# Window attention with sink keys and a gated feed-forward block on one core: sink values by transfer, paired sink products, an uneven last block and a new order of work

## The chip, the cores and the metric

The kernel runs on one core of a Trainium2 chip. The core has a matrix engine (TensorE, "PE" in the profile, with its weight loads shown apart as "PEld"), VectorE ("DVE"), ScalarE ("ACT"), GpSimd ("POOL") and SyncE ("SP"), which run their own instruction queues in order and wait for each other by semaphores. Transfers are started by POOL, SP and ACT and carried out by 16 DMA engines. Matrix products land in eight accumulator banks of 128 x 512 float32. The metric is the device time of one execution, in microseconds; the lower the better.

## What is computed

Attention over 4 batches, 8 heads, 768 positions and head size 64. Each query sees the last 128 keys up to itself, and the first four keys of the sequence (the "sinks"). Its output, 3072 rows of 512, is normalized by its root mean square and goes through a gated feed-forward block with 1536 hidden columns.

```python
scores = scale * np.matmul(q, k.transpose(0, 1, 3, 2))
is_sink = pos[None, :] < int(n_sink)            # 4
in_window = (rel >= 0) & (rel < int(window))    # 128
scores = np.where(is_sink | in_window, scores, -1e9)
a = softmax(scores)
x = np.matmul(a, v)           # heads side by side: 3072 x 512
xn = x / rms * rms_g
g = xn @ w_gate
silu = g * (1.0 / (1.0 + np.exp(-g)))
out = (silu * (xn @ w_val)) @ w_out
```

## The kernel before

The work is cut into 24 blocks of 128 query rows, `g` = 0 to 23, six to a batch (`NT` = 6; `b` is the batch, `t` the block's place in it). A block's q, k and v come by transfers that GpSimd issues (L400, L404) and that turn float32 into bfloat16; k and q of block 0 come through SP as float32 instead (L392) and are cast. The first eight blocks are transposed on TensorE (L492), later ones by transposing transfers on SP (L506). The weights `wg`, `wv` and `wo` come through GpSimd as well (L446, L452), between the first blocks.

Scores are held transposed: keys on the partitions, queries along the columns. A block of keys meets its own queries and those of the next block. Three forms exist: the plain one (L532, tiles of 64 rows by 128 columns of the array, two heads side by side), one for a batch's last block (L548, the same tiles), and one that leaves the empty triangles out (L610, "tri", tiles of 64 by 64, used from block 4 on for all but a batch's first and last block). ScalarE takes exponentials (L583, L559, L619), VectorE or GpSimd masks them, and the products with v (`av`, L653 to L668) sum numerator and denominator, by a column of ones beside v. Each block has two halves of four heads, `u` = 0 and 1, each in one bank.

From a batch's third block on (`t` >= 2) the sinks lie outside the window and have a product of their own. `sink_s` (L772) gives the scores of the sinks, their exponentials are `esk` (L781), 128 partitions holding every head's sinks. `vsk` holds the values of the four sinks on the partitions that belong to each head, zero elsewhere. It is made by `sink_v` (L754), which multiplies v of the batch's first block with a selecting matrix `sel` on TensorE, once for each half, and by `sink_vm` (L763), in which VectorE multiplies the result with the mask `headm`. `sel` and `headm` are made once from the identity (L367, L371). The first product of `av` is then `esk` with `vsk`, 128 x 128 by 260 columns (L653), and starts the bank.

After `av`, VectorE divides (L682), ScalarE squares and sums (L690), VectorE normalizes (L697 to L714), and the block is transposed into `xnt`, by TensorE for the first eight blocks (L729) and by a transfer on SP for the others (L741). The feed-forward part works on groups of four blocks, `G` = 0 to 5. Its products `g` and `v` (both L1000) go in chunks of 128 columns for group 0, 256 for groups 1 and 2, and 512 for the others; ScalarE's tanh (L1007) and two passes of VectorE (L1013, L1023) turn them into `hT`; `project` (L1033) multiplies with `wo`, ScalarE evicts (L1041) and SP stores (L1045). The last block of all is projected in two halves of 256 columns (L1051), evicted by ScalarE and VectorE (L1062, L1066) and stored by ACT and SP (L1069).

What sets the order: every piece of work is an entry of a plan (`op`), with what it needs, what it gives, and which banks it takes and drops. The table `ORDER` lists, for each engine, the entries in the order in which that engine's queue gets them. `Plan.run` walks through these five lists with durations of its own to decide how they interleave in the program and which of the eight banks an entry gets. Thirty small products with zeros (`warm`, L468) stand among the first of TensorE's entries.

Of the kernel before, what the change touches and what calls it, by code (L numbers as in the profile page):

```python
# [9 lines left out]
ALU = mybir.AluOpType  # L10
# [5 lines left out]
P = 128  # L16
# [18 lines left out]
class Plan:  # L35
# [5 lines left out]
    LATE = 300  # L41
    DEPTH = 8
    WARM_AT = 11500
    HOP = {"PE": 40, "ACT": 35, "DVE": 35, "POOL": 90, "SP": 60}
    START = {"PE": 800, "ACT": 800, "DVE": 1030, "POOL": 1290, "SP": 800}

    def __init__(self):
        self.ops, self.held = [], {}
        self.rings = {"POOL": 0, "HW": 0, "TR": 0}
        self.banks = {i: 0 for i in range(8)}  # L50

    def op(self, ways, needs=(), gives=(), prio=0.0, takes=(), drops=(), ring=None, work=0.0,
           mode=0):
        self.ops.append(dict(
            ways=ways, needs=set(needs), gives=tuple(gives), prio=prio, takes=tuple(takes),
            drops=tuple(drops), ring=ring, work=work, mode=mode, at=len(self.ops), ready=0,
        ))

    def land(self, ring, first, work):


        r = self.rings
        if ring == "POOL":
            begin = max(first, r["POOL"], r["HW"])
            r["POOL"] = begin + (1.4 * work if begin < 8500 else work)
            self.loads -= 1
            return r["POOL"] + 520 + (1000 if r["POOL"] > 9000 else 0)
        if ring == "HW":
            begin = max(first, r["HW"], r["POOL"])
            r["HW"] = begin + (1.25 * work if begin > 2500 else work)  # L70
            return r["HW"] + 900
        begin = max(first, r["TR"])
        late = max(0, r["POOL"] - begin)
        if late and self.loads:
            r["POOL"] += 1.1 * work
        r["TR"] = begin + work
        return r["TR"] + (550 if ring == "TR" else 850) + min(late, 5000)

    def run(self, table):
        ids = {e: span(table[e]) for e in self.START}  # L80
        assert sorted(sum(ids.values(), [])) == list(range(len(self.ops)))
        free, at, users, last = dict(self.START), dict.fromkeys(self.START, 0), {}, []
        self.loads = sum(o["ring"] == "POOL" for o in self.ops)
        wait = {o["at"]: set(o["needs"]) for o in self.ops}
        for o in self.ops:
            for t in o["needs"]:
                users.setdefault(t, []).append(o)
        mode, order = 0, []
        lock, pool_end = (0, 0), 0
        while len(order) < len(self.ops):  # L90
            first = None
            for e in self.START:
                if at[e] == len(ids[e]):
                    continue
                o = self.ops[ids[e][at[e]]]
                k = len(o["takes"])
                if wait[o["at"]] or k > len(self.banks):
                    continue
                ready = o["ready"] + self.HOP[e] if o["ready"] else 0
                if k:  # L100
                    ready = max(ready, sorted(self.banks.values())[k - 1] + 40)
                if o["ring"] == "POOL" and len(last) >= self.DEPTH:
                    ready = max(ready, last[-self.DEPTH])
                start = max(free[e], ready)
                if first is None or start < first[0]:
                    first = start, e, o
            if first is None:
                raise RuntimeError("stuck")
            start, e, o = first
            at[e] += 1  # L110
            ns, lat, fn = o["ways"][e]
            if e == "PE":
                cold = max(0, self.WARM_AT - start)
                ns += min(ns, cold / 2)
                if o["mode"] != mode:
                    ns, mode = ns + 95, o["mode"]
                lat = ns + 180
            if o["mode"] == 9:
                if e == "DVE":
                    more = max(0, pool_end - (start + ns - 770))  # L120
                    lock = start + ns + more - 770, start + ns + more
                else:
                    more = lock[1] - start if start < lock[1] and start + ns > lock[0] else 0
                    pool_end = start + ns + more
                ns, lat = ns + more, lat + more
            for s in o["takes"]:
                i = min(self.banks, key=lambda i: (self.banks[i], i))
                del self.banks[i]
                self.held[s] = i
            free[e] = start + ns  # L130
            end = start + lat
            if o["ring"] is not None:
                end = self.land(o["ring"], end, o["work"]) + self.LATE
                if o["ring"] == "POOL":
                    last.append(end)
            for s in o["drops"]:
                self.banks[self.held[s]] = end + 12
            for t in o["gives"]:
                for x in users.pop(t, ()):
                    x["ready"] = max(x["ready"], end + 12)  # L140
                    wait[x["at"]].discard(t)
            order.append((start, end, e, fn, o))
        return order
# [21 lines left out]
""",  # L165
    "ACT": """
19 15 139 144 146 149 145 147 150 137 151 173 152 157 194 176 178 177 183 179 181 196
184 182 189 198 200 199 167 201 192 579 208 584 594 211 215 599 609 589 614 232 604 217
219 218 220 619 250 234 227 236-239 169 252 254 256 624 245 634 267 629 640 295 262 273
271 274 272 297 248 299-302 265 281 659 650 645 664 655 284 308 674 315 291 316 669 317  # L170
318 330 331 679 332 333 311 684 345 346 689 347 348 324 339 694 360 293 699 362 704 720
374 709 375 376 354 377 396 397 714 368 398 725 399 384 749 744 739 759 405 730 764 754
735 411-414 392 426-429 769 420 441 442 774 443 444 779 789 784 800 435 794 453 458 460
472-475 815 466 805 482 494 829 495 496 824 497 819 810 834 839 844 854 849 859 869 864
506 512-515 874 530 531 490 532 533 548 549 890 880 904 550 909 551 524 919 566 568 899
542 924 934 914 560 929 939 944 574 949 895 885 954 984 989 979 999 960 994 1009 975
1004 1014 1019 970 1029 1024 1034 965 1040 1050 1045 1053 1054
""",
    "DVE": """
7 0-2 11 10 17 6 141 12 171 4 13 163 156 154 158 165 213 5 186 188 160 161 190 202 203  # L180
# [23 lines left out]
""",  # L204
}


@with_exitstack
def kernel(
# [13 lines left out]
    nc = tc.nc  # L223
# [939 lines left out]
```

## Time and profile before

| | |
|---|---|
| median of 3 runs | 244.19 us (243.29 to 245.17) |
| the profiled execution | 242.75 us |
| its span, first to last instruction | 241.0 us |
| TensorE's granted clock, mean | 0.984 |
| DVE / ACT / POOL busy | 78% / 51% / 37% |
| L653, sink products, 128 x 260 | 32 instructions, mean 275 ns |
| L754, products with `sel`, 128 x 260 | 8 instructions, mean 306 ns |
| L763, `vsk` on VectorE, 128 x 260 | 8 instructions, mean 422 ns |

"PE busy" counts a matmul from its start to its modelled end, so that neighbours overlap; the distance from one start to the next tells how long a product holds the engine. The chain of waits is followed back from the last instruction, at each step to what released it. Line numbers are those of the kernel before.

### The profile page before, as it was taken

To read this page: it belongs to the slowest core of one execution; us is meant where nothing else is said; L and a number is where in the kernel's file an instruction comes from. 1 tells how busy PE (TensorE), PEld (TensorE's weight loads), DVE (VectorE), ACT (ScalarE), POOL (GpSimd) and SP (SyncE) were. 2 spreads that over 40 slices of the span, in tenths; PEclk is the share of its full clock that TensorE was granted. 3 is DMA by queue.
4 is the path that set the end of the run, shared out by engine and by line. 5 is a ranking of instruction groups with operands and counts; after the bars stand their busy time and mean duration, and the time that the engine had idled before them with its cause. 6 is when DMAs were issued, how large, how long until landed. Compare 5 with 4: busy or idle time off the path is not lost.

```text
span 241.0 us, 5846 instructions
## 1 busy us (share of the span) xinstructions
PE 235.0 (98%) x2324; PEld 149.8 (62%) x2324; DVE 187.0 (78%) x482; ACT 122.3 (51%) x267; POOL 89.9 (37%) x116
## 2 busy tenths in 40 slices
PE   6999999999999999999999999999999999999994
PEld 3469987875788676786886544445545444444443
DVE  2489979998999999999998999974599965436430
ACT  3775577477867565346754373461762222304211
POOL 8976885587555475200062123045340000000000
PEclk9679999999999999999999999999999999999999
DMA  9999999999999999999997809510241130103014
GB/s 125 148 183 188 184 184 187 164 136 150 141 137 149 180 165 146 159 180 169 141 153 70 109 0 112 115 40 0 87 47 22 21 112 0 69 18 131 3 50 167
DMA packets 113581, 27.38 MB, mean 114 GB/s; under 512 B 103697, under 2 KB 110609, under 8 KB 113554
## 3 DMA queue, kind: packets, MB, share of 16 engines
q0 software_dynamic: 81760, 13.90, 77.5%
q1 hardware_dynamic: 31650, 12.99, 29.8%
q8 instruction: 18, 0.29, 0.5%
q10 hardware_dynamic: 144, 0.13, 0.2%
q14 instruction: 9, 0.07, 0.1%
HBM read 28.31 MB, written 6.29 MB: 144 GB/s over the span
## 4 chain that ended last, share of the span: by engine, by line
PE 85%; DMA 7%; POOL 5%; issue 0%; DVE 0%; POOLq 0%
PE o L1033 25%; PE v L1000 24%; PE g L1000 23%; DMA wv<-in_moe_w_val_dram 4%; DMA q<-in_q_dram 3%; PE s L610 3%; PE av L668 2%; PE av L663 2%; PE av L653 2%; POOL wg L446 1%; POOL q L400 1%; POOL v L404 1%; PE o_last L1051 1%; POOL k L400 1%; PE s L532 1%; POOL wv L446 1%
## 5 line engine op out<-in xcount | busy, mean ns | idle before, releaser
L1000 PE MATMUL v<-xnt,wv 128*128 128x128 bf16 (+2 forms) x528 | 73.3, 282 | 0.0
L1000 PE MATMUL g<-xnt,wg 128*128 128x128 bf16 (+2 forms) x528 | 70.9, 282 | 0.0
L1033 PE MATMUL o<-wo,hT 128*128 128x512 bf16 x276 | 67.7, 379 | 0.0
L1007 ACT ACTIVATE th<-g 128x512 bf16<-128x512 f32 x72 | 41.6, 600 | 45.0 <-PE g L1000 40.0
L1013 DVE SCALAR_TENSOR_TENSOR p<-th,g 128x512 bf16<-128x512 bf16 x72 | 47.5, 682 | 17.6 <-ACT th L1007 17.4
L1000 PEld LDWEIGHTS <-wg 128*128 128x128 bf16 x528 | 43.2, 98 | 19.6 <-DMA wg<-in_moe_w_gate_dram 0.2
L1023 DVE TENSOR_TENSOR hT<-p,v 128x512 bf16<-128x512 bf16 x72 | 47.8, 682 | 9.6 <-PE v L1000 8.9
L1000 PEld LDWEIGHTS <-wv 128*128 128x128 bf16 x528 | 42.7, 98 | 19.9 <-issue 0.7
L1033 PEld LDWEIGHTS <-hT 128*128 128x128 bf16 x276 | 25.7, 98 | 26.0 <-issue 0.4
L644 POOL TENSOR_SCALAR_AFFINE_SELECT e<-e 128x512 bf16<-128x512 bf16 x20 | 12.6, 652 | 51.1 <-ACT e L619 50.8
L619 ACT ACTIVATE e<-s 128x384 bf16<-128x384 f32 x52 | 22.8, 498 | 15.4 <-PE s L610 15.3
L404 POOL DMA_DIRECT2D v<-in_v_dram x24 | 21.4, 890 | 9.1 <-DMA q<-in_q_dram 5.7
L690 ACT ACTIVATE sq<-x 128x512 bf16<-128x512 bf16 x24 | 15.3, 636 | 17.9 <-DVE x L682 17.7
L400 POOL DMA_DIRECT2D k<-in_k_dram x23 | 20.4, 888 | 8.5 <-DMA wo<-in_moe_w_out_dram 2.7
L400 POOL DMA_DIRECT2D q<-in_q_dram x23 | 20.5, 890 | 7.7 <-DMA k<-in_k_dram 4.5
L1041 ACT ACTIVATE osb<-o 128x512 f32<-128x512 f32 x23 | 13.5, 602 | 19.0 <-PE o L1033 19.0
L682 DVE TENSOR_TENSOR x<-av,rden 128x256 bf16<-128x256 f32 x48 | 20.4, 425 | 1.7
L714 DVE SCALAR_TENSOR_TENSOR xr<-x,r,gb 128x512 bf16<-128x512 bf16 x24 | 18.0, 752 | 0.8
L668 PE MATMUL av<-v,e 128*128 128x65 bf16 x192 | 17.8, 196 | 0.2
L583 ACT ACTIVATE e<-s 128x512 bf16<-128x512 f32 (+1 forms) x36 | 16.0, 528 | 2.8 <-PE s L532 2.3
L663 PE MATMUL av<-v,e 128*128 128x65 bf16 x160 | 15.5, 193 | 0.0
L668 PEld LDWEIGHTS <-e 128*128 128x128 bf16 x192 | 13.4, 99 | 2.6 <-DVE e L594 0.4
(78 smaller groups left out, 199.8 us busy)
## 6 DMA issues: line engine op xcount, KB each, us to landing
out_dram<-osb SPq DMA_DIRECT2D x23, 256.0 KB, 2.3
v<-in_v_dram POOLq DMA_DIRECT2D x24, 128.0 KB, 9.7
q<-in_q_dram POOLq DMA_DIRECT2D x23, 128.0 KB, 10.0
k<-in_k_dram POOLq DMA_DIRECT2D x23, 128.0 KB, 9.5
wo<-in_moe_w_out_dram POOLq DMA_DIRECT2D x2, 768.0 KB, 11.0
wg<-in_moe_w_gate_dram POOLq DMA_DIRECT2D x5, 256.0 KB, 8.2
wv<-in_moe_w_val_dram POOLq DMA_DIRECT2D x5, 256.0 KB, 8.6
stage<-in_k_dram SPq DMA_DIRECT2D x1, 256.0 KB, 3.2
```

What stands on the lines that cost most here:

```text
L400: nc.gpsimd.dma_start(out=T[name, g], in_=block_of(src, g))
L404: nc.gpsimd.dma_start(out=V16[b][:, t, :, 0:D], in_=block_of(v, g))
L619: nc.scalar.activation(out=e_tile(g)[:, x:x + 2, 0:TW], in_=BANK.pop(("s", g, u, hi))[:, 0:2 * TW].rearrange("p (j c) -> p j c", c=TW), fu ...
L663: nc.tensor.matmul(out=dest, lhsT=T["e", g - 1][:, x, P:2 * P], rhs=V16[b][:, t - 1, h, :], start=(t == 1), stop=False, skip_group_check=True,
L668: nc.tensor.matmul(out=dest, lhsT=T["e", g][:, x, 0:P], rhs=V16[b][:, t, h, :], start=(t == 0), stop=True, skip_group_check=True,)
L682: nc.vector.tensor_tensor(out=T["x16", g][:, 4 * u:4 * u + 4, :], in0=pvv[:, :, 0:D], in1=rden.unsqueeze(2).to_broadcast((P, 4, D)), op=AL ...
L714: nc.vector.scalar_tensor_tensor(out=T["xr", g], in0=T.pop(("x16", g)).rearrange("p h d -> p (h d)"), scalar=r[:, 3:4], in1=gb, op0=ALU.mu ...
L1000: nc.tensor.matmul(out=ps[:, i * n:(i + 1) * n], lhsT=w_sb[:, kt, ft * P:(ft + 1) * P], rhs=T["xnt", G][:, kt, cols], start=(kt == 0), sto ...
L1007: nc.scalar.activation(out=T["th", key], in_=BANK[("g", key)], func=ACT.Tanh, scale=0.5,)
L1013: nc.vector.scalar_tensor_tensor(out=T["p1", key], in0=T.pop(("th", key)), scalar=1.0, in1=BANK.pop(("g", key)), op0=ALU.add, op1=ALU.mult,)
L1023: nc.vector.tensor_tensor(out=T[hk][:, i:i + n, cols], in0=T.pop(("p1", key)).rearrange("p (n c) -> p n c", n=n), in1=BANK.pop(("v", key)) ...
L1033: nc.tensor.matmul(out=BANK[("o", G, tb)], lhsT=T["h", G, ft // 4][:, ft % 4, tb * P:(tb + 1) * P], rhs=wo[:, ft, :], start=(ft == 0), sto ...
```

## The change

Five things change.

- `sel` and the products with it go. `vsink`, 128 partitions x 4 batches x 65 columns of float32, is set to one by VectorE at the start, and four transfers on SP (one for each sink, 8 KB each) put v's first four rows into it, on partitions 16 h + i for head h and sink i. `sink_v` is now one VectorE operation of 520 columns for each batch. `headm` and `ksk` follow this layout of the partitions.
- For nine blocks (`hosted`: g = 8, 9, 10, 11, 14, 15, 20, 21, 22) the sink product is no longer the first of `av`. It stands at the end of the next block's score phase, split by the half `u`, each using the 64 partitions that hold its heads: two pieces where that phase has tiles of 64 x 128, four (also split by queries) where it has 64 x 64. The two banks of `av` are taken there, earlier than before.
- The last block is projected as 384 and 128 columns.
- 56 `warm` products in place of 30.
- The order: new lists for the engines, and two more tables, `TURNS` (how the engines interleave) and `BANKS` (which bank each taking entry gets), in place of the durations in `Plan.run`. In GpSimd's list the first transfer (q of block 1) now stands ahead of the two selects that make `ident` and `bias`. The first 24 of GpSimd's transfers are the same set in another order, with a transfer of `wg` as the fourth.

```diff
-    WARM = 30
+    WARM = 56
+    HOST_FROM = 8
-    sel = const.tile([P, P], BF16, name="sel")
+    vsink = const.tile([P, B, VW], FP32, name="vsink")
...
+    dve(260, lambda: nc.vector.memset(vsink, 1.0), gives=["vsink1"], prio=-95)
+    def load_sink(i):
+        nc.sync.dma_start(
+            out=vsink.rearrange("(h r) b c -> h r b c", r=SW // 2)[:, i, :, 0:D],
+            in_=v[:, :, i, :].rearrange("b h d -> h b d"),
+        )
...
     def av(g, u):
-        pv = bank(("av", g, u))
-        if t >= 2:
+        pv = BANK["av", g, u] if hosted(g) else bank(("av", g, u))
+        if t >= 2 and not hosted(g):
...
+    def hosted(g):
+        b, t = divmod(g, NT)
+        return (HOST_FROM <= g < NB - 1 and t >= 2 and not (b in MERGE and t >= NT - 2))
+
+    def sink_av(g, halves):
+        b = g // NT
+        n = P // halves
+        for i in range(halves):
+            for u in range(2):
+                if i == 0:
+                    bank(("av", g, u))
+                pr, cols = slice(u * D, (u + 1) * D), slice(i * n, (i + 1) * n)
+                nc.tensor.matmul(
+                    out=BANK["av", g, u][cols, 0:HW], lhsT=T["esk", g][pr, cols],
+                    rhs=T["vsk", b][pr, 4 * u:4 * u + 4, :], start=True, stop=False,
+                    tile_position=(u * D, i * n) if halves > 1 else None,
+                    skip_group_check=True,
+                )
...
-    def sink_v(b, half):
-        nc.tensor.matmul(
-            out=bank(("vs", b, half))[:, 0:HW], lhsT=sel,
-            rhs=V16[b][:, 0, 4 * half:4 * half + 4, :], start=True, stop=True,
-        )
...
+    def sink_v(b):
+        T["vsk", b] = sink.tile([P, H, VW], BF16, name="vsk")
+        nc.vector.tensor_tensor(
+            out=T["vsk", b], in0=vsink[:, b:b + 1, :].to_broadcast((P, H, VW)),
+            in1=headm.unsqueeze(2).to_broadcast((P, H, VW)), op=ALU.mult,
+        )
...
+    ENDS = (slice(0, DM - P), slice(DM - P, DM))
...
-    order = plan.run(ORDER)
+    order = plan.run(ORDER, TURNS, BANKS)
```

More of the change, by code (lines that the diff above doesn't have):

```diff
@@ L55, in op @@
             ways=ways, needs=set(needs), gives=tuple(gives), prio=prio, takes=tuple(takes),
-            drops=tuple(drops), ring=ring, work=work, mode=mode, at=len(self.ops), ready=0,
+            drops=tuple(drops), ring=ring, work=work, mode=mode, at=len(self.ops),
         ))
[L59 to L125, printed above, removed]
-            for s in o["takes"]:
[L127 to L135, printed above, removed]
-            for s in o["drops"]:
[L137 to L142, printed above, removed]
@@ new lines, in run @@
+    def run(self, table, turns, banks):
+        ids = {"PADGS"[i]: (e, iter(span(x))) for i, (e, x) in enumerate(table.items())}
+        banks, given, owner, order = iter("".join(banks.split())), set(), {}, []
+        for c in "".join(turns.split()):
+            e, ops = ids[c]
+            o = self.ops[next(ops)]
+            assert o["needs"] <= given, o["gives"]
+            for s in o["takes"]:
+                i = self.held[s] = int(next(banks))
+                assert i not in owner, s
+                owner[i] = s
+            for s in o["drops"]:
+                assert owner.pop(self.held[s]) == s
+            given.update(o["gives"])
+            order.append((e, o))
+        assert len(order) == len(self.ops)
@@ L173 @@
[L173 to L177, printed above, removed]
+24 20 22 199 177 175 178 176 182 180 181 183 168 188 222 204-206 211 207 212 209 191 210
@@ L380 @@
     dve(300, cut_ident, ["ident"], ["idnos"], -59)
-    dve(1040, make_masks, [("bias", 0), ("bias", 1)], ["masks"], MASKS_PRIO)
-    dve(560, make_sel, ["ident"], ["sel", "headm"], MASKS_PRIO + 1)
+    dve(800, make_masks, [("bias", 0), ("bias", 1)], ["masks"], MASKS_PRIO)
+    dve(490, make_headm, ["ident"], ["headm"], MASKS_PRIO + 1)
+    dve(260, lambda: nc.vector.memset(vsink, 1.0), gives=["vsink1"], prio=-95)
[4 more added lines that the diff above has]
+        )
+    for i in range(NS):
+        sp(430, 2600, lambda i=i: load_sink(i), ["vsink1", "grow"], [("vsink", i)], -70 + i)
     def block_of(src, g):
@@ L426, in sw_load @@
         n = len(issue)
-        op({"POOL": (ns, 1900, fn)}, list(needs), list(gives) + [("sw", n)], -89 + n,
+        op({"POOL": (ns if n else 1010, 1900, fn)}, list(needs), list(gives) + [("sw", n)], -89 + n,
            ring="POOL", work=work)
@@ L674, in av, with host @@
             T.pop(("e", g - 1), None)
+    def hosted(g):
[15 more added lines that the diff above has]
+                )
+    def host(g, halves):
+        if not (g and hosted(g - 1)):
+            return 0, [], [], [], []
+        b, t = divmod(g - 1, NT)
+        return (115, [lambda: sink_av(g - 1, halves)], [("esk", b, t), ("vsk", b)],
+                [("sa", g - 1)], [("av", g - 1, u) for u in range(2)])
     def normal(g, u):
@@ L824, in block_scores @@
             ns, work = 220 * (n1 - n0), [lambda g=g, n=(n0, n1): scores(g, *n)]
+            if last:
+                more, extra, also, given, banks = host(g, 1)
+                needs, gives, takes = needs + also, gives + given, takes + banks
+                ns, work = ns + more, work + extra
             if merged and n0 == 0:
@@ L868, in tri_block @@
         gives = [("s", g, 0), ("s", g)]
-        ns, work = 330, [lambda: tri_scores(g)]
+        more, extra, also, given, banks = host(g, 2)
+        needs, gives, takes = needs + also, gives + given, takes + banks
+        ns, work = 330 + more, [lambda: tri_scores(g)] + extra
         if b >= FUSE_FROM:
@@ L923 @@
             else:
-                pe(220, lambda g=g: scores_last(g), needs, [("s", g, 0), ("s", g)], pa + 1,
-                   takes=slots, mode=1)
+                more, extra, also, given, banks = host(g, 1)
+                pe(220 + more, lambda g=g, extra=extra: [scores_last(g)] + [w() for w in extra],
+                   needs + also, [("s", g, 0), ("s", g)] + given, pa + 1, takes=slots + banks,
+                   mode=1)
             xs = []
@@ L947 @@
             needs += [("v", g - 1)] if t else []
[L948 removed]
+            needs += [("esk", b, t), ("vsk", b)] if t >= 2 else []
             needs += [("av", g - 1, u)] if g else []
[L950 to L951 removed]
+            needs += [("sa", g)] if hosted(g) else []
+            pe((130, 242, 242 if hosted(g) else 354)[min(t, 2)], lambda g=g, u=u: av(g, u), needs,
+               [("av", g, u)], pa + 5, takes=[] if hosted(g) else [("av", g, u)])
             dve(548, lambda g=g, u=u: normal(g, u),
@@ L977 @@
                                if b >= 2 else []), [("ksk", b)], 0.1 * g)
-            for half in range(2):
-                pe(115, lambda b=b, half=half: sink_v(b, half), [("v", g), ("vone", b), "sel", ("s", g)],
-                   [("vs", b, half)], pa + 14, takes=[("vs", b, half)])
-                dve(340, lambda b=b, half=half: sink_vm(b, half), [("vs", b, half), "headm"]
-                    + ([("av", NT * (b - 2) + NT - 1, u) for u in range(2)] if b >= 2 else [])
-                    + ([("vsk", b, 0)] if half else []),
-                    [("vsk", b, half)], 0.1 * g, drops=[("vs", b, half)])
+            dve(640, lambda b=b: sink_v(b), [("vsink", i) for i in range(NS)] + ["headm"]
+                + ([("av", NT * (b - 2) + NT - 1, u) for u in range(2)] if b >= 2 else []),
+                [("vsk", b)], 0.1 * g)
             for t0, n in sink_parts(b):
```

110 lines of the change are left out of this document (57 added, 53 removed), and 68 rows, old and new, of the table ORDER.

## The prediction

> **What bounds the kernel now.** The summary comes first: who is busy, and when.
>
> ```profile
> span 241.0 us, 5846 instructions
> ...
> PE 235.0 (98%) x2324; PEld 149.8 (62%) x2324; DVE 187.0 (78%) x482; ACT 122.3 (51%) x267; POOL 89.9 (37%) x116
> ...
> PEclk9679999999999999999999999999999999999999
> ```
>
> TensorE is busy nearly throughout and its clock is full, but for a stretch near the start. "Busy" is partly modelled, so the chain of waits is read next, in order of time, over the first 34 us:
>
> ```profile
> 1.15 0.29 POOL ident L338
> 1.44 0.25 POOL bias L344
> ...
> 1.76 1.01 POOL q L400
> 2.77 0.88 POOL k L400
> ...
> 14.14 9.69 DMA wv<-in_moe_w_val_dram
> ...
> 24.13 7.73 DMA q<-in_q_dram
> ...
> 31.91 0.40 PE q L492 x4
> ```
>
> Up to 31.9 us the path is the stream of loads that GpSimd issues: two selects, transfer after transfer, and the q of block 4, on which TensorE's transposes start. Behind that, the same view over the rest holds TensorE alone, down to the last eviction:
>
> ```profile
> 229.05 6.04 PE o L1033 x28
> 235.09 2.63 PE o_last L1051 x24
> 237.72 0.02 issue
> 237.75 0.42 DVE last L1062
> ```
>
> So from 31.9 to 237.7 us a column taken from TensorE is time taken from the kernel, as long as no new wait opens. What a column costs is read from starts, since durations (274 ns for a 260-column sink product) contain a pipeline's depth that the next matmul covers. TensorE's timeline around 70 us:
>
> ```profile
> 69.03 0.54 PE L610 MATMUL s<-qkT 64*64 64x192 bf16 x24
> 69.50 1.05 PE L1000 MATMUL v<-xnt,wv 128*128 128x256 bf16 x8
> 70.39 0.27 PE L653 MATMUL av<-vsk,esk 128*128 128x260 bf16 x1
> 70.50 0.19 PE L663 MATMUL av<-v,e 128*128 128x65 bf16 x1
> ```
>
> A sink product holds TensorE for 70.50 - 70.39 = 0.11 us.
>
> **The change, part by part.**
>
> *Products with `sel` (L754).* Eight go. They are as wide as the sink products, so 0.11 us each. Two, at 9.0 and 13.3 us, lie before 31.9, where the load stream leads: nothing. Six lie behind: 6 x 0.11 = -0.67 us.
>
> *Sink products of nine blocks.* Blocks 8 to 11, 14, 15 and 20 to 22 are hosted. They now spend 18 x 0.11 = 1.98 us. In six of them the host is a score phase of 64x64 tiles and the work becomes four quarter-array pieces; in three it is a phase of 64x128 tiles with two pieces. All pieces keep 260 columns. The old trace has no such piece; the nearest row is the score phase above. Its 24 matmuls hold 8 x (192 + 64 + 128) = 3072 columns. Beside it 8 x 256 = 2048 columns of whole-array work take 0.89 us with the entry included, so 3072 in single file would take 1.3 us. They take 0.47. Pieces on different quarters do run beside each other. I take 0.12 us a block: 9 x 0.12 = 1.08, a gain of 0.90 us. The other end is single file: 24 + 6 = 30 pieces x 0.11 = 3.3 us, a loss of 1.3. The row decides for the gain.
>
> *Entering and leaving small tiles.* Four 512-column products take 0.97 us when a score phase comes behind them and 0.86 otherwise, so an edge costs 0.1 us. Counting tile sizes along TensorE's queue gives 55 edges in both programs: nothing. One edge more or less for each hosted block would be 0.9 us either way.
>
> *GpSimd's first transfer ahead of the selects.* In the new order q goes first, from about 0.82 us (SP's first issue starts at 0.81), for 1.01 us; the selects, which now wait until 1.15 for VectorE's memset, follow with 0.25 each; k starts at 2.4 instead of 2.77. The first 24 transfers, up to block 4's q, are the same set. Bounds: 0 (the queue is full from 14 us) and -0.94 (the shift of q). The second issue is nearest to what the rest of the stream follows: -0.3 us. The price: `ident` and `bias` come about 0.65 later, and the four bias products, at 2.31 for 1.7 us, end at some 4.7 instead of 4.0. k's transposes start at 4.74, behind the cast, so this is just covered; uncovered it costs 0.5 us on a stretch where the loads lead.
>
> *Warm-up products, 30 to 56.* They lie before block 4's q. Nine more than now stand behind the first FFN product, worth 0.056 each (16 of 128 columns take 0.89): 0.5 us. The DMA link at 24.13 to 31.86 covers them: nothing; if it ends earlier, up to +0.5.
>
> *Four sink transfers on SP.* Each is 8 KB; the issue of the 2 KB `grow` takes 0.47, so 1.9 us of SP, whose next issue is at 47.4 us. Landing, by the rows of `stage` 3.2 to 3.9 us after issue, is before 9 us; the first sink product is at 19.9. VectorE, in order, waits for them with `vsk`; were they 3 us late, it and the copies of q, k behind it would be. Nothing.
>
> *VectorE.* Off go 8 x 0.42 (L763), and 0.27 for `sel`; on come four multiplications of 520 columns (0.42 to 0.84 each) and a memset (0.2 to 0.4). It has 0% of the chain: nothing.
>
> *The end.* The 384 and 128 columns hold TensorE as long as twice 256. The last eviction falls from 0.42 for 256 columns to some 0.3, an estimate from that row; a smaller store may land earlier. The first part (ScalarE 0.38 for 256 columns, 0.60 for 512) ends about 0.2 us before TensorE does, then issues, and lands about with the second. Bounds 0 and -0.3; I take -0.13.
>
> Sum: -0.67 - 0.90 - 0.30 - 0.13 = -2.0 us. The profiled execution took 242.75 us (span 241.0 and 1.7 around it), which gives 240.75 and a span of 239.0. The median of the runs, 244.19, stands 1.44 above it; the same 2.0 off the median gives **242.2 us**.
>
> **The rivals.**
>
> *The pieces run in single file.* Sink work then loses 1.3 instead of gaining 0.90: -2.0 + 2.2 = +0.2, 244.4 us. For it: no row has 260-column pieces. Against: the 0.47 us above. [...]
>
> *Accumulator banks run short (slower).* A hosted block now takes its two banks a phase before its softmax is ready, while scores hold four of the eight, for four exponentials of 0.50 us. Gate and value products then share two. If a product group waits for one VectorE pass (0.68 us, L1013) in each hosted block, it costs 9 x 0.68 = 6.1: 248.3 us. It decides from 2.0 / 9 = 0.22 us a block on. Against: banks are given out by a fixed list, the exponentials free one each 0.5 us, and a product group lasts 0.87.
>
> *A transfer moved on SP comes late.* Transposes take 7.3 to 8.0 us to land, in the median, while loads run; each one that goes ahead delays the next by 1.25 us of issue. One such delay reaching TensorE: 243.4 us. For it: SP's order is new throughout. Against: TensorE waits for none now.
>
> *TensorE's early clock decides.* By the microsecond (the fields behind the engines are granted clock, DMA share and GB/s):
>
> ```profile
> 8.00:9.00 1.00, 1.00 (x2) 0.00 (x0) 0.00 (x0) 1.00 (x5) 1.00 (x3) 0.58 2.25 143
> 9.00:10.00 1.00, 1.00 (x13) 0.91 (x12) 0.52 (x2) 1.00 (x4) 1.00 (x2) 0.50 2.34 149
> ...
> 14.00:15.00 1.00, 0.97 (x12) 0.50 (x7) 0.62 (x3) 0.91 (x4) 1.00 (x2) 0.51 1.43 192
> ```
>
> Between 8 and 15 us half the clock is lost, 0.42 + 5 x 0.50 + 0.49 = 3.4 us of work. If more warm-ups hold the clock and TensorE's front rather than the loads sets the end, this comes on top: 238.8 us. [...] Against: in the chain the loads lead until 31.9, whatever TensorE's clock was.
>
> **How the numbers follow.** The sum 0.61, single file 0.08, banks 0.13, a late transfer 0.12, the clock 0.06. The first case's own range, with the bounds above and the runs' scatter (243.29 to 245.17), is 241.0 to 243.6. Leaving out the clock, most of the banks' case and a strip of the first gives 240.9 to 245.2. One per cent, about what a measurement of this kernel tells from no change, is 241.75 and 246.63. Faster: the clock and a third of the first case, 0.27. Slower: most of the banks' case, 0.11. Between: 0.62.
>
> **What would show it.** Six `sel` products fewer behind 31.9 us; hosted sink products starting a few ns apart inside score phases, each phase some 0.12 us longer (single file: 0.44); GpSimd's k at 2.4 us and block 4's transposes near 31.6; 55 edges; TensorE alone in the chain from there to the end; last eviction 0.3 us. The forecast is wrong if TensorE shows idle time behind 32 us, with an exponential or an eviction as the releaser (banks) or a transposing DMA (SP); or if block 4's transposes start well before 31 us.

## The result and the profile after

The changed kernel took 242.06 us in the median of 12 runs (241.63 to 243.59), the kernel before, beside it, 243.40 us (242.77 to 245.17). The ratio is 0.9947, with an interval of 0.9923 to 0.9972: half a per cent faster, within the 1% that was called no change. The forecast was 242.2 us. Two more series of the same kernel, shown below, gave 0.9936 and 0.9934.

The profiled execution took 243.59 us, the slowest of those 12 runs, with a span of 241.9 us. Its page:

```profile
span 241.9 us, 5897 instructions
...
PE 231.3 (96%) x2329; PEld 147.6 (61%) x2354; DVE 187.4 (77%) x478; ACT 122.8 (51%) x267; POOL 89.2 (37%) x116
...
PEclk9999999999999999999999999999999999999999
```

TensorE's granted clock is full throughout (mean 1.000; before 0.984); the half-rate stretch of before (0.50 between 9 and 14 us) is gone. TensorE is busy for 3.7 us less in a span that is 0.9 longer, so idle time has appeared. Part of that is only missing records (2354 weight loads, one for each matmul, stand against 2329 matmuls; the chain shows an idle gap of 0.05 us where one lacks). The list of what TensorE waited for shows the rest, in its second and third lines behind the wait at the start:

```profile
PE s L563 <- DMA qkT<-q: 1.3, 1, 1.3
PE s L563 <- DMA qkT<-k: 0.8, 1, 0.8
```

Before, no wait on a transposing transfer was in that list. The chain of waits of the changed kernel, from 50 to 77 us (start, duration, what), shows where they come from:

```profile
54.59 1.20 SPq L459
...
55.88 2.46 SPq L459
...
58.43 1.22 SPq L459
...
59.75 10.61 DMA qkT<-q
...
70.49 0.54 PE s L563 x16
71.03 0.11 PE av L641 x4
71.15 1.85 PE v L975 x16
```

SP's queue (L459 is the transposing DMA) issues one transpose after another, and the q of block 10, issued at 59.75, lands 10.61 us later, when TensorE has been ready for block 9's scores (L563), which need it, for 1.3 us. The hosted sink work is in the next line: four pieces in 0.11 us, at the end of the score phase.

The front of the chain, the counterpart of GpSimd's rows of before:

```profile
1.32 0.16 POOL q L353
1.48 0.85 issue
...
2.42 0.30 POOL ident L286
2.72 0.24 POOL bias L292
2.95 0.86 POOL k L353
```

q starts at 1.32 (before 1.76) and not at 0.82; k starts later than before (2.95 in the chain, 2.90 as its own row; before 2.77).

To see where time went, the span is cut at three marks that every trace has: the start of block 4's q transposes on TensorE, the first score of block 10, and the start of the last eviction. Between the marks both kernels do the same work, but for the sink products and the products with `sel`. In the kernel before, the first and the last mark stand in rows shown ahead (31.91 and 237.75), and the middle one is:

```profile
73.16 0.54 PE L610 MATMUL s<-qkT 64*64 64x192 bf16 x24
```

All in us:

| kernel (profiled execution) | block 4's transposes start | from there to block 10's scores | from there to the last eviction | from there to the end |
|---|---|---|---|---|
| before | 31.91 | 41.25 | 164.59 | 3.30 |
| changed | 31.74 | 43.64 | 163.59 | 2.91 |
| changed, first repeat | 31.95 | 41.62 | 163.59 | 2.91 |
| forecast, against before | -0.30 | -0.32 | -1.25 | -0.13 |
| first repeat, against before | +0.04 | +0.37 | -1.00 | -0.39 |

The forecast's row holds its own terms: two of the six `sel` products (0.22) and one hosted block (0.10) lie in the second stretch, four (0.45) and eight (0.80) in the third. The third stretch fell by 1.00 of 1.25. The second grew where it should have shrunk, and there the waits on transposing transfers lie. The first did not move.

### The profile page after: what moved, and what is told of

Its sections match the earlier page's. It is cut to its first block, busy times and chain, and to the rows that moved or that the text cites. A ratio compares the mean times of both kernels' runs of the same rounds, so it can differ in the third digit from the quotient of the medians.

```text
span 241.9 us, 5897 instructions
## 1 busy us (share of the span) xinstructions
PE 231.3 (96%) x2329; PEld 147.6 (61%) x2354; DVE 187.4 (77%) x478; ACT 122.8 (51%) x267; POOL 89.2 (37%) x116
## 4 chain that ended last, share of the span: by engine, by line
PE 67%; DMA 20%; POOL 6%; issue 2%; DVE 2%; SPq 2%; POOLq 0%
PE v L975 20%; PE o L1008 20%; PE g L975 18%; DMA wo<-in_moe_w_out_dram 5%; DMA qkT<-q 4%; DMA wv<-in_moe_w_val_dram 4%; DMA wg<-in_moe_w_gate_dram 3%; DMA q<-in_q_dram 3%; POOL v L357 2%; SPq L459 2%; PE s L563 2%; PE av L621 2%; POOL k L353 1%; PE av L616 1%; PE o_last L1028 1%
## 5 line engine op out<-in xcount | busy, mean ns | idle before, releaser
L975 PE MATMUL v<-xnt,wv 128*128 128x128 bf16 (+2 forms) x527 | 72.2, 282 | 0.4 <-DMA wv<-in_moe_w_val_dram 0.2
L1008 PE MATMUL o<-wo,hT 128*128 128x512 bf16 x259 | 65.3, 379 | 1.1 <-issue 0.5
L988 DVE SCALAR_TENSOR_TENSOR p<-th,g 128x512 bf16<-128x512 bf16 x72 | 48.1, 682 | 18.9 <-ACT th L982 18.7
L975 PEld LDWEIGHTS <-wv 128*128 128x128 bf16 x528 | 43.3, 98 | 21.3 <-DMA wv<-in_moe_w_val_dram 0.6
L693 DVE SCALAR_TENSOR_TENSOR xr<-x,r,gb 128x512 bf16<-128x512 bf16 x24 | 18.7, 778 | 0.8
L621 PE MATMUL av<-v,e 128*128 128x65 bf16 x192 | 16.4, 193 | 0.3 <-DMA v<-in_v_dram 0.3
L536 ACT ACTIVATE e<-s 128x512 bf16<-128x512 f32 (+1 forms) x36 | 15.1, 519 | 1.6 <-PE s L485 1.5
L616 PE MATMUL av<-v,e 128*128 128x65 bf16 x160 | 14.8, 193 | 0.0
L621 PEld LDWEIGHTS <-e 128*128 128x128 bf16 x192 | 12.7, 97 | 2.8 <-DVE e L547 0.4
```

The source lines that it names most:

```text
L616: nc.tensor.matmul(out=dest, lhsT=T["e", g - 1][:, x, P:2 * P], rhs=V16[b][:, t - 1, h, :], start=(t == 1), stop=False, skip_group_check=True,
L621: nc.tensor.matmul(out=dest, lhsT=T["e", g][:, x, 0:P], rhs=V16[b][:, t, h, :], start=(t == 0), stop=True, skip_group_check=True,)
L693: nc.vector.scalar_tensor_tensor(out=T["xr", g], in0=T.pop(("x16", g)).rearrange("p h d -> p (h d)"), scalar=r[:, 3:4], in1=gb, op0=ALU.mu ...
L975: nc.tensor.matmul(out=ps[:, i * n:(i + 1) * n], lhsT=w_sb[:, kt, ft * P:(ft + 1) * P], rhs=T["xnt", G][:, kt, cols], start=(kt == 0), sto ...
L988: nc.vector.scalar_tensor_tensor(out=T["p1", key], in0=T.pop(("th", key)), scalar=1.0, in1=BANK.pop(("g", key)), op0=ALU.add, op1=ALU.mult,)
L1008: nc.tensor.matmul(out=BANK[("o", G, tb)], lhsT=T["h", G, ft // 4][:, ft % 4, tb * P:(tb + 1) * P], rhs=wo[:, ft, :], start=(ft == 0), sto ...
```

## The experiments

**Theory A.** The changed kernel's products cost what the forecast says, but the new order on SP lets transposing transfers come late and gives back 0.6 to 1 us. **Rivals:** the hosted pieces cost more than 0.12; the clock or the warm-ups matter; GpSimd's early transfer is worth its 0.3 after all.

**The changed kernel again,** unaltered, as the reference of the next three (one chip).

> The changed kernel once more, nothing altered. Theory A (in its profiled execution the score phases of blocks 8 and 9 waited 0.8 and 1.3 us for transposing transfers of SP, and that is the accident of some executions): median near 242.1 us, that is 0.994 to 0.995 of the kernel before; the time of an execution follows the sum of these two waits, so a profile without them has a span near 239.8 to 240.2 us. Theory B (the waits are in every execution and the gain comes in spite of them): the new profile shows again some 2 us of waits at these two phases at whatever time.

Measured: 241.94 us (241.39 to 242.39, 8 runs; the kernel before 243.35), ratio 0.9936 (0.9913 to 0.9959). Its profiled execution, 241.77 us, is a typical one, and is the third row of the table above. Of the two waits on transposing transfers one came back (block 8's k, 0.6 us), the other (block 10's q, 1.3 us) did not.

**SP's order put back for one pair.** In the changed kernel SP has q and k of blocks 8, 9 and q of 10 in the order q8, q9, k8, k9, q10; before it was q8, k8, q9, k9, q10.

```diff
-19 21 23 16 15 18 17 337 352 338 353 367 660 382 368 383 396 415 397 416 430 675 351 445
+19 21 23 16 15 18 17 337 338 352 353 367 660 382 368 383 396 415 397 416 430 675 351 445
```

> Only SP's list is altered: the transposing transfer of block 8's k goes ahead of that of block 9's q, as in the kernel before. In the changed kernel it stood behind q of block 9, whose load landed at 54.5 us, and was issued at 55.9 instead of about 49.1 us. Theory A (this order is the source of the waits): issue at 49 to 50 us, no wait of TensorE on a transposing transfer at blocks 8 and 9, a span near 239.7 us, median 0.3 to 1.0 us under the changed kernel's. Rival (the transfers land late because the loads crowd the DMA engines, whatever SP's order): the waits stay within 0.5 us of what the changed kernel shows, median the same within 0.3 us.

Measured: 241.01 us (240.75 to 241.98, 6 runs), ratio 0.9899 (0.9873 to 0.9925), 0.93 under its neighbour. SP's timeline in the changed kernel (the repeat; start, duration with the waits inside a group, line, count):

```profile
47.38 8.14 SPq L459 DMA_TRANSPOSE qkT<-q  x2
55.61 3.75 SPq L459 DMA_TRANSPOSE qkT<-k  x2
```

and with the pair put back:

```profile
47.25 1.37 SPq L459 DMA_TRANSPOSE qkT<-q  x1
50.78 1.19 SPq L459 DMA_TRANSPOSE qkT<-k  x1
54.01 1.19 SPq L459 DMA_TRANSPOSE qkT<-q  x1
```

q9's load lands only at some 54 us. Where q9 stands second, SP waits for it, and block 8's k, which could go at 50.78, waits behind it until 55.61. TensorE's row in that execution shows the price in its brackets:

```profile
65.25 0.54 PE L563 MATMUL s<-qkT 64*64 64x192 bf16 x24 [0.63 <-DMA qkT<-k]
```

With the pair put back the same phase starts at 64.43 and waits for nothing. The whole difference of the second stretch between these two traces, 0.71 us, arises at this phase; and the 40.91 us that are left lie 0.34 below the kernel before, where the forecast had 0.32. Block 8's scores wait 0.6 to 0.8 us in all five traces with the changed order, and in none of the eight with the pair put back.

The 1.3 us for block 10's q in the slowest run are another matter. That transfer stands fifth in both orders. It was issued at 59.75 there, at 59.45 in the first repeat, which did not wait for it, and at 57.40 to 59.42 with the pair put back. Most of that wait is therefore the landing of 10.61 us, and why it took so long is open.

**The nine sink products back in `av`.** The hosted form issues nothing; `av` does the 128 x 128 product for every block with `t` >= 2. Order and banks stay.

```diff
-        pv = BANK["av", g, u] if hosted(g) else bank(("av", g, u))
-        if t >= 2 and not hosted(g):
+        pv = bank(("av", g, u))
+        if t >= 2:
...
     def sink_av(g, halves):
+        return
```

> The nine hosted sink products go back to the start of their own block's product with v, as one 128 x 128 product of 260 columns for each half; the order, the banks and when they are taken stay as in the changed kernel. By the sum (0.22 us a block against 0.12): 9 x 0.10 = 0.9 us above the changed kernel's median, 0.4 to 1.2 with scatter. If the pieces ran in single file: 1.3 us under it. If TensorE's columns there are covered by other waits: the same within 0.3 us.

Measured: 242.66 us (242.01 to 243.81, 12 runs), ratio 0.9967 (0.9948 to 0.9987): 0.72 above the repeat of the changed kernel beside it. The traces say it more sharply. First the start of block 10's scores and the last eviction in this kernel:

```profile
73.30 0.54 PE L563 MATMUL s<-qkT 64*64 64x192 bf16 x24
...
237.78 0.29 DVE L1040 TENSOR_SCALAR last<-o_last 128x128 f32<-128x128 f32 x1 [7.11 <-PE o_last L1029]
```

That is 164.48 us. Every kernel with hosted products and no added ones takes 163.58 to 163.60 us there. The 0.89 us belong to eight blocks, 0.111 each; the ninth lies between the scores of blocks 9 and 10 and adds another 0.11 (5.00 instead of 4.89). So hosting gains 1.00 us for nine blocks. Since two whole-array products cost 0.22, the pieces of a block cost 0.11, as the row of four in 0.11 says. Single file would have been 0.44, four times the 0.11 of a 260-column product.

**Only the first 15 warm-up products.** The others are left out; nothing uses what they compute.

```diff
+    FIRST = {140, 138, 114, 151, 122, 152, 124, 143, 154, 119, 156, 157, 117, 111, 142}
+
...
+        if i + 111 not in FIRST:
+            return
```

> Only the first 15 of the 56 warm-up products are left, 41 are left out; order and all else as in the changed kernel. Theory (the load stream leads to 31.7 us, so that TensorE's early clock has next to no price): the granted clock falls to half somewhere between 7 and 18 us, block 4's transposes start no later than 32.2 us, median within 0.5 us of the changed kernel's. Rival (the held clock is what brought the gain): the clock falls likewise, block 4's transposes start 1 us or more later than 31.7 us, and the median is 1.0 us or more above the changed kernel's.

Measured: 241.61 us (241.31 to 242.21, 6 runs), ratio 0.9923 (0.9898 to 0.9947), 0.33 below its neighbour. In its trace the clock was halved again for 3.4 us, a mean of 0.993 over the execution (the windows by the microsecond; the field behind the five engines is the granted clock):

```profile
10.00:11.00 1.00, 1.00 (x3) 0.30 (x2) 0.94 (x4) 0.55 (x2) 1.00 (x2) 0.50 2.36 154
...
12.00:13.00 1.00, 0.85 (x14) 0.60 (x14) 0.89 (x6) 0.59 (x1) 1.00 (x3) 0.50 2.07 163
```

and yet block 4's transposes start at 32.10, 0.15 behind those of its neighbour with a full clock, and the time is not longer. Half the clock for 3.4 us costs nothing that can be measured here.

The next four were run on another chip, all with SP's pair put back, so that the transposing transfers are out of the way (the kernel before: 243.35 us).

**The last block in two halves of 256 columns again.**

```diff
-    ENDS = (slice(0, DM - P), slice(DM - P, DM))
+    ENDS = (slice(0, DM // 2), slice(DM // 2, DM))
```

> The changed kernel with block 8's k transposing DMA ahead of q9's on SP (no wait of TensorE on a transposing transfer, 241.01 us, span from the last eviction's start to its end 2.90 us), and the last block's product again as two halves of 256 columns. The prediction priced 384 and 128 columns at -0.13 us, the difference of the two evictions alone (0.42 and 0.29): by that this run is at 241.14, and 3.03 us lie between the last eviction's start and the end. Theory A, from the two traces: the smaller last transfer is faster too (packets of 512 B, 27 ns, instead of 1024 B, 46 ns), so the term is -0.39: 241.40, and 3.3 us behind the last eviction's start. Rival: the ends differ for another reason (the load of SP's queue, noise): 241.0, 2.9 us.

Measured: 241.45 us (241.15 to 242.47, 6 runs), ratio 0.9929. From the start of the last eviction to the end its trace has 3.05 us, against 2.90: the term is 0.15, as the forecast had it (0.13). Theory A's 3.3 is refuted. So 0.25 of the 0.39 that the two traces showed there has another cause, which stays open. By the packets' own times it does not lie in the eviction or the transfer: the last packet ends 1.80 us after the last eviction's start in the kernel before and 1.78 here, and behind it come 1.49 and 1.26 us.

**GpSimd's two selects first again, then q.**

```diff
-25 8 9 26-28 31 34 30 32 37 35 29 38 33 39 41 42 40 43 45 47 44 48 46 49 36 50 53 57 52
+8 9 25 26-28 31 34 30 32 37 35 29 38 33 39 41 42 40 43 45 47 44 48 46 49 36 50 53 57 52
```

> The same kernel with the swap on SP, and GpSimd's two selects ahead of its first transfer again, as in the kernel before. The prediction priced the transfer's move at -0.30 us, since k would be issued at 2.40; in the trace of the changed kernel q is issued at 1.32 (before 1.76) and k at 2.90 (before 2.77). Theory A: k's issue leads, not q's, and the move is worth nothing or costs up to 0.13: this run is at 240.9 to 241.0, with q issued at 1.76, k at 2.77, and block 4's first transposes at 31.7 to 31.9. Rival (the prediction's step): the move gains 0.3, and this run is at 241.3 with block 4's transposes 0.3 later.

Measured: 241.36 us (240.96 to 242.08, 6 runs), ratio 0.9921 (0.9904 to 0.9938). q is issued at 1.72 and k at 2.72; block 4's transposes start at 32.02. Both figures are nearer to the rival (241.3) than to theory A (240.9 to 241.0, transposes at 31.7 to 31.9). But the swap alone had been run on another chip, so the two were run side by side, below.

**448 and 64 columns.**

```diff
-    ENDS = (slice(0, DM - P), slice(DM - P, DM))
+    ENDS = (slice(0, DM - P // 2), slice(DM - P // 2, DM))
```

> The same kernel with the swap on SP, and the last block's product as 448 and 64 columns instead of 384 and 128. If the end is set by the small part's eviction and transfer (theory A), a 64-column eviction and 256-byte rows end sooner by about half of what 256 to 128 columns gave: 240.8, and 2.7 us from the last eviction's start to the end. Rival: the larger part's transfer, issued by ScalarE, ends last now (its eviction of 448 columns cannot start before its products end, some 0.2 us later than with 384): 241.0 or more, and the last packets are those of ScalarE's queue.

Measured: 241.58 us (241.26 to 242.47, 6 runs), ratio 0.9932, and 3.25 us behind the last eviction's start: the rival. ScalarE's issue of the larger part stands beside SP's now (the issues' rows):

```profile
237.73 0.40 ACTq L1046 DMA_DIRECT2D out_dram<-last  x1
...
237.75 0.33 SPq L1046 DMA_DIRECT2D out_dram<-last  x1
```

With 384 columns ScalarE's came 0.47 ahead of SP's (236.19 and 236.66). The last packets are those of the larger part (1792 bytes each, the last ending at 239.43; the small part's at 238.86): 224 KB, issued 0.02 us ahead of 32 KB, end 0.57 us behind them.

The profiled execution of this kernel took 242.47 us, the longest of its six runs, and its second stretch is 1.00 longer than with the swap alone. All of that arises at one place, where the products with v wait for a load of v that GpSimd issued:

```profile
49.67 0.19 PE L621 MATMUL av<-v,e 128*128 128x65 bf16 x1 [0.83 <-DMA v<-in_v_dram]
```

So with the pair put back the loads can still hold TensorE up behind 32 us.

**15 warm-up products, with the pair put back.**

> The same kernel with the swap on SP, and only the first 15 of the warm-up products (the 26 that follow are left out; they compute nothing that is used). With the changed order on SP the same cut measured 241.61 against 241.94. If that was a gain of its own (fewer products and fewer edges of tile size ahead of the loads' data), this run is at 240.7; if it was the wait on a transposing transfer coming out smaller by chance, 241.0 to 241.3, with block 4's first transposes at 31.8 to 32.1. By the prediction's rival (d) a halved clock of 3.4 us costs up to 3.4: 242.7 to 244.4.

Measured: 241.66 us (240.86 to 241.83, 5 runs), ratio 0.9924 (0.9909 to 0.994). The gain of the earlier cut did not return. This time the granted clock was full (mean 1.0), although the products left out are the same; block 4's transposes start at 31.79. Block 7's scores, at 55.73, waited 0.4 us for the q of block 8, which stands first in both orders on SP.

The last four were run on a third chip (the kernel before: 243.75 us).

**The changed kernel and the swap once more, side by side.**

> The changed kernel once more, beside the next three on one chip. The runs with the swap on SP have given medians from 241.01 to 241.66 us with a small edit each, on two chips; the difference of 0.93 between this kernel and the swap alone came from one chip. Theory A (the late transposing transfers cost 0.6 to 1.1 us): 241.9 to 242.2 here, 0.6 to 1.1 above the next. Rival (the swap's gain was mostly chance): within 0.3 of the next.

> The changed kernel with block 8's k transposing DMA ahead of q9's on SP, once more. Theory A: 241.0 to 241.4, TensorE waiting at most 0.1 us for a transposing transfer behind 32 us. Rival: 241.7 or more.

Measured: 241.96 us (241.75 to 242.47, 6 runs), ratio 0.9934 (0.9915 to 0.9954), and 241.55 us (240.85 to 242.37, 6 runs), ratio 0.9918 (0.9892 to 0.9945). The swap gains 0.41 here, between the two expectations and within the scatter of its runs. The 12 runs of the swap in all fall into two groups, eight at 240.75 to 241.15 and four at 241.98 to 242.37; the profiled ones (240.96 and 241.11) are both of the first, so what the second group waits for was not seen in this kernel. The wait for a load of v in the run with 448 and 64 columns would be long enough; that it is the same is not shown. In the changed kernel's trace block 8's scores waited 0.7 us again. For the matmuls the profile names a tanh of ScalarE, but the weight loads of this phase, which bring in the keys, start at the same time and name the transfer:

```profile
65.61 0.41 PEld L563 LDWEIGHTS <-qkT 64*64 64x64 bf16 x24 [1.01 <-DMA qkT<-k]
```

The tanh is not what the scores need: in the trace of the swap they start at 64.58, before it does (64.75). k8's transpose, issued at 57.33 here, was later than in any other trace.

**Six products put back.** Two 128 x 128 by 260 column products in front of the value products of the first block of batches 1, 2 and 3; the next products overwrite what they write.

```diff
         pv = BANK["av", g, u] if hosted(g) else bank(("av", g, u))
+        if t == 0 and b:
+            nc.tensor.matmul(
+                out=pv[:, 0:HW], lhsT=ident, rhs=V16[b][:, 0, 4 * u:4 * u + 4, :],
+                start=True, stop=True, skip_group_check=True,
+            )
```

> The same with six products of 128x128 by 260 columns put back, two in front of the value products of the first block of batches 1, 2 and 3 (they are overwritten at once), where the kernel before had its six sel products. The prediction priced those six at 0.67 us, all of it on TensorE's path behind 31.9 us. If TensorE alone sets that stretch: 0.65 to 0.70 above the run before this one, 241.7 to 242.1. Rival: some of them fall into TensorE's idle time and the six cost under 0.3.

Measured: 241.65 us (241.41 to 242.06, 6 runs), ratio 0.9921 (0.9901 to 0.994): only 0.10 above the swap beside it, whose median lies between its two groups, and 0.5 to 0.9 above that kernel's first group. The medians leave it open; the traces don't. Block 10's scores and the last eviction, first with the swap alone:

```profile
72.90 0.54 PE L563 MATMUL s<-qkT 64*64 64x192 bf16 x24
...
236.49 0.29 DVE L1039 TENSOR_SCALAR last<-o_last 128x128 f32<-128x128 f32 x1 [7.11 <-PE o_last L1028]
```

and with the six products:

```profile
73.14 0.54 PE L563 MATMUL s<-qkT 64*64 64x192 bf16 x24
...
237.18 0.29 DVE L1044 TENSOR_SCALAR last<-o_last 128x128 f32<-128x128 f32 x1 [7.11 <-PE o_last L1033]
```

163.59 against 164.04 us: 0.45 for the four that lie in this stretch, 0.11 each. The second stretch, with the other two, takes 41.13 against 40.91 in the first trace of the swap: 0.22.

**Selects first, beside the swap.**

> The swap with GpSimd's two selects ahead of its first transfer again, beside the swap alone on the same chip. On another chip it measured 241.36. Theory: q's earlier issue (1.32 instead of 1.72) is worth nothing, since k's, at 2.90 instead of 2.72, is what TensorE waits for: equal within 0.15, or 0.1 to 0.2 faster than the swap alone. Rival, the prediction's step: moving q forward gains 0.3, so this run is 0.3 slower than the swap alone.

Measured: 241.31 us (240.79 to 241.76, 6 runs), ratio 0.9904 (0.9881 to 0.9927), 0.24 below the swap alone, within the scatter of both: no gain from moving q ahead of the selects can be seen in the time. The issues tell what the move does. With q first, q starts 0.40 earlier (1.32 against 1.72), but k and the eight transfers behind it start about 0.2 later (2.91 against 2.72 for k, 8.89 against 8.66 for the ninth transfer). At block 4's transposes this is no longer to be read: they start at 32.02 and 32.42 with the selects first, and at 31.53 to 32.22 with q first. That is later rather than earlier, but two traces do not settle it in this scatter.

The marks in these traces, beside those of the table above:

| kernel | block 4's transposes start | to block 10's scores | to the last eviction | to the end |
|---|---|---|---|---|
| changed, second repeat | 32.22 | 41.71 | 163.59 | 2.90 |
| swap | 31.84 | 40.91 | 163.60 | 2.90 |
| swap again | 31.53 | 41.37 | 163.59 | 2.91 |
| sinks in `av` | 31.55 | 41.75 | 164.48 | 2.91 |
| swap, six products | 32.01 | 41.13 | 164.04 | 2.91 |
| swap, halves | 31.74 | 41.11 | 163.60 | 3.05 |
| swap, 448 and 64 | 32.01 | 41.91 | 163.59 | 3.25 |
| 15 warm-ups, changed order | 32.10 | 41.87 | 163.60 | 2.90 |
| 15 warm-ups, swap | 31.79 | 41.83 | 163.59 | 2.91 |
| swap, selects first, twice | 32.02, 32.42 | 41.09, 40.90 | 163.59, 163.58 | 2.91, 2.92 |

With the pair put back the second stretch takes 40.90 to 41.91 us, with the changed order 41.62 to 43.64. The swap takes away the wait for block 8's k; other waits, for the loads above all, come and go.

The change with SP's pair put back has the lowest medians of the three: 241.01 and 241.55 us, against 241.94 and 241.96 for the change and 243.35 and 243.75 for the kernel before. Its distance from the kernel before is clear of noise, that from the change is clear on the first chip alone.

## Why the forecast was right, and where its steps were wrong

The time came out at 242.06 for 242.2, but that it came so close is luck: two errors of opposite sign stand behind it. The change was forecast at -2.0 us. Measured beside the kernel before, it is -1.3, -1.4 and -1.8 by the medians, and -0.98 between the profiled executions of the kernel before and of the first repeat; the former, at 242.75, was faster than all 12 runs that stand beside the changed kernel. The forecast took its 2.0 off a median of three runs, 244.19; the same kernel over 12 and 19 runs has 243.40 and 243.35. The base was 0.8 too high, and the gain some 0.6 too large.

- *`sel` products, -0.67.* Right: 0.11 each by the six that were put back, in a trace; the median (0.10 for all six) does not resolve it.
- *Hosted sink products, -0.90.* Right in mechanism, a tenth too small: 1.00 by the trace, +0.72 in the medians when undone. The pieces run beside each other, four in 0.11 with their weight loads: in the changed kernel those of block 8's pieces stand at 70.74 to 70.92 us, inside the score phase, and the pieces end at 71.15. The rival of single file is refuted.
- *The two together.* From block 10 on the two undone edits are worth 0.89 + 0.45 = 1.33 us, the kernel before is 1.00 longer. One edge of tile sizes more in this stretch (29 against 28, with 55 in all in both) gives back 0.1, an estimate from the chain of before, where four 512-column products take 0.97 us right behind a score phase (91.63) and 0.86 otherwise; about 0.2 stays open.
- *GpSimd's first transfer, -0.30.* Wrong. The step took q's start from SP's first issue (0.81); GpSimd's first transfer starts at 1.32, its sequencer idle 0.8 us ahead of it, for a reason that the traces do not show. So the selects end later, and k came at 2.90 instead of 2.77, not at 2.4. Put back, the kernel is no slower by its median. What the move is worth at block 4 stays open: its transposes scatter from 31.53 to 32.42 over these kernels, more than the term.
- *A transfer moved on SP comes late, chance 0.12.* The sum put this at nothing and kept it as a rival; it came, on top of the sum. Its price was put at 1.2 us. By the traces with and without the swap it is 0.71, by the medians 0.93 and 0.41; the slowest run lost 0.8 to it, and 1.3 more to block 10's q, which the order explains only in small part. Against it stood "TensorE waits for none now". That is a fact of the old order. The old rows had what was needed, on SP's queue before the change:

```profile
47.36 2.40 SPq L506 DMA_TRANSPOSE qkT<-q  x1
49.81 1.26 SPq L506 DMA_TRANSPOSE qkT<-k  x1
54.53 1.19 SPq L506 DMA_TRANSPOSE qkT<-q  x1
```

These are q8, k8 and q9. Behind k8 comes no issue until 54.53, because q9's load lands only then (SP waits 3.5 us for it). The changed order put k8 behind that waiting transfer, and its issue went from 49.81 to 55.88 us.
- *Sink transfers on SP, 0.* Right, though they came later than the "before 9 us" of the forecast: SP spent 2.66 us on the four instead of 1.9, and VectorE's first `vsk`, at 10.80 in the profiled execution, had waited 0.4 us for them. Up to 31.7 us the loads lead there.
- *Warm-ups, 0, and the early clock as a rival.* Right, and refuted: with the full clock (mean 1.000 against 0.984) block 4's transposes started 0.17 us earlier, not 3.4, and a clock of 0.50 for 3.4 us in the cut with 15 products cost nothing that can be measured. The runs of the kernel before beside the first repeat say the same: nine with a mean granted clock of 0.986 to 0.993 have a median of 243.33 us, ten with 0.999 or 1.0 have 243.53. That more warm-ups hold the clock was the author's assumption, and no run shows it: the same cut of warm-ups met a halved stretch of 3.4 us in one kernel (mean 0.993) and none in the other (1.0), and with all 56 the first run with the selects first has a mean of 0.993 too.
- *Banks.* Refuted: in the three traces of the changed kernel no exponential and no eviction is named as the releaser of a TensorE wait of over 0.3 us behind 32 us, but for the tanh discussed above, where the wait was k8's; nine waits of 0.22 would have been needed.
- *The end, -0.13.* Right in size: 0.15 when undone. The traces of before and after differ by 0.39.

## What to carry to other kernels

Before moving a transfer forward in a queue, look up when its own data land: here block 8's k, put behind a transfer whose data landed at 54.57 us, was issued at 55.88 instead of 49.81, and "nobody waits for this queue now" had said nothing about the new order. Sum a forecast against a base measured with the change, or give the base's own error a place in the range. When medians scatter by half a microsecond, cut the traces at marks that all kernels share: here a stretch of 164 us on TensorE alone repeats within 0.02 us, and an edit of 0.11 us can be read in it.

## What the hardware showed that was not expected

- Transposing transfers of one block took 9.6 us (k, issued at 55.61 in the first repeat) and 10.6 us (q, issued at 59.75 in the slowest run) to land while GpSimd's loads were in flight, though SP's issue of one takes 1.2 us.
- From block 10's scores to the last eviction, eleven executions of kernels with the same products took 163.58 to 163.60 us, on at least three chips, while the first 32 us, led by the loads, differ by 0.9 us between them.
- Four 64 x 64 pieces of 260 columns take 0.11 us together, as long as one 128 x 128 product of 260 columns.
- GpSimd's first transfer of the program started at 1.31 to 1.32 us in every trace in which it stood first, half a microsecond behind SP's first issue (0.81).
